# Sliding-window attention beside a GELU layer: the first chunk's logits copied from PSUM bank by bank, and another order of the pieces

## The chip, the core and the metric

The kernel runs on one core of a Trainium2 chip. The metric is the device time of one execution in microseconds (us), the median of several runs. The engines of the core are TensorE (PE in the profile, its weight loads PEld), VectorE (DVE), ScalarE (ACT), GpSimd (POOL) and SyncE (SP, which here issues DMA transfers). Each works through its own list of instructions in order and waits on semaphores for the others.

## The reference

The input `x` has 2048 rows of 640 numbers in bf16. It is normalised (`xn`), and the output is the sum of `x`, an attention over a few earlier rows, and a dense layer with GELU:

```python
xn = layernorm(x)                                  # [2048, 640]
q, k, v = split(xn @ wqkv)                         # 32 heads of 20 numbers
# row s looks at the 8 rows s, s-2, ..., s-14 of its own head
logits[h, s, w] = (q[h, s] . k[h, s - 2*w]) * 20**-0.5     # -1e9 where s - 2*w < 0
attn = softmax(logits, over w)
o[h, s] = sum over w of attn[h, s, w] * v[h, s - 2*w]
out = x + o @ wo + gelu(xn @ w1 + b1) @ w2 + b2    # w1: 640 x 1536, w2: 1536 x 640
```

## The kernel before

The 2048 rows are cut into four chunks of 512, and each chunk into four blocks of 128. The program is made of 626 named pieces, and the list `ORDER` at the top of the file gives the order in which they are emitted. Each engine keeps that order for its own instructions; nothing reorders them later. Semaphore waits are put in by the framework where a piece uses what an earlier one wrote. In a piece's name the first digit is the chunk.

The pieces that matter here:

- `st`, `rs`, `rc`, `xn`: statistics of the rows (VectorE L213, L215, for chunks 2 and 3 ScalarE passes `su` L225 and `sq` L232 that write to a scratch tile `trash`), the reciprocal deviation on ScalarE (L244, L247) and the normalised rows. `tp`, `tc` turn them so that columns lie on partitions (`xnT`).
- `ho`, `wa`, `wb`, `tb`: at the start, a small table for the heads, matmuls that fill time, and the bias rows turned through TensorE.
- `pj` (L333) and, for chunk 0, `ga` to `ge` and `hj` (L346, L377): the projections to `qT`, `kT`, `vT`. TensorE adds them up in PSUM, four banks in turn, shared with the GELU layer's first product. `pc`, `gc`, `hc` copy them out on ScalarE (L397, L370, L392), and each such copy frees a bank. `pad` (L402 to L406) copies the last 14 columns of the chunk before in front of `kT` and `vT`; `pad11` (L404) is that of chunk 1's `kT`.
- `qk` (L430): VectorE multiplies a block's queries by the eight shifted windows of keys into the big tile `prod`. `pa`, `pb` (L465, L471) fold it, and `lg` (L480) sums it over a head's numbers on TensorE: the logits `L`, a PSUM tile of [128, 8 offsets, 128] in f32, which is two banks, offsets 0 to 3 in one and 4 to 7 in the other. There are four such products, one a chunk; "first logits" and "second logits" are those of chunks 0 and 1.
- the softmax: `cp` copies `L` to the bf16 tile `e`; `mask`; `m` and `mx` find and subtract the maximum (L527, L529, L538); `ex` is the exponential on ScalarE (L543); `ss` the sum (L527, L529); `ri` its reciprocal as a logarithm and an exponential on ScalarE (L552, L553); `at` the product (L558), named `attn`. The exponentials and logarithms use another table of ScalarE than GELU, so a table load (L170) stands between them. Chunk 0 does all this in two halves `a` and `b` of 64 columns (`PARTS`), the other chunks in one.
- `xe`: transfers on SP that spread `attn` to all rows of a head. `av`, `ac`, `ad`, `ot` (L584 to L607): the weighted sum of values.
- `f1` (L614) and `ge` (L630): the GELU layer's first product and GELU, to `hT`. `t` (L696) turns the second product and the output projection into the tile `T`, `u` (L699) adds the bias, `ut` turns it by DMA and `ud` (L708) adds it to the output in DRAM, to which `xp` (L300) wrote `x` before. The last chunk ends in another way: `o` (L652), `dl`, `dh` (L664) and `dd`; `xb` adds its bias rows into `x`.
- `ldx`, `ld2`, `ldo`: loads on SP of later rows of `x`, of `w2` and of `wo`.

In chunk 0 `cp0b` is a VectorE copy of columns 64 to 127 of all eight offsets, and `cp0a` a ScalarE copy of columns 0 to 63 of all eight, so each reads from both banks. In the order they stand as `cp0b cp0a`.

Of the kernel before, what the change touches and what calls it, by code (L numbers as in the profile page):

```python
# [16 lines left out]
S, D, F, H, W, DIL = 2048, 640, 1536, 32, 8, 2  # L17
# [14 lines left out]
PARTS = (2, 1, 1, 1)  # L32
# [5 lines left out]
COLS = ((0, 2), (2, 4), (4, 5))  # L38

ORDER = """  # L40
pad01 pad02 st00a st00 sum1 ho rs00 neg1 xn00a sq1 xn00b tp00a wa tp00b wb tc00a tc00b rs01 ga xn01a gb2 xn01b tp01a
gb3 st02a tb tp01b tc01a gb4 st02 tc01b gd gc0 st03a ge rs02 st03 hj101 b1 xn02 rs03 gc4 xn03 gc1 tp02 st12a tp03
hc101 st11a hj100 tc03 st10a st12 tc02 hj102 st13a hc100 hj010 st10 hc102 st13 hj200 st11 rs1 hj110 hc200 rc1 qk01
xn10 hj012 hc110 tc10 hj011 pk xn11 hj111 hc012 tc11 hc010 qk00 hc011 hj112 hc111 f10_2 hc112 xn13 f10_0 xn12 tc13
qk02 f10_1 tc12 ge0_0 f10_5 ldx qk03 f10_11 ge0_5 f10_3 ge0_11 ge0_2 pj101 ge0_3 pa00 pj112 pc101 ge0_1 pj104 pc112
xp2 pa01 su20 pj110 xp0 pc104 ld2 su22 pj102 pc110 pb01 pj100 su21 hj201 su23 pc102 pb04 pj103 ng2 pc100 hc201 pj114
sq22 lg0 pc114 ldo pj111 cp0b cp0a sq21 mask pj113 m0b pc103 m0a pj124 pc111 mx0a pc113 mx0b t000 pad11 qk11 pj120
ex0b hj202 ex0a hj210 pc120 sq23 ss0a hj211 pc124 ss0b sq20 pj122 qk13 hc202 rs2 f10_7 hc211 pc122 t040 ri0b f10_8
ri0a rc2 qk12 hc210 f10_4 f11_1 ge0_7 xn21 qk10 f11_3 ge0_4 tc21 xn20 pj121 ge1_3 tc20 t041 ge1_1 pa11 f11_9 ge0_8
xn23 hj212 pc121 tc23 t001 xn22 pa10 f10_6 hc212 tc22 ge1_9 f11_10 ge0_6 at0a at0b f10_9 ge1_10 pb11 xe01 su33 xe03  # L50
t002 xe00 ge0_9 pj123 pad21 su32 pb14 pj210 xe02 su31 pj203 xp1 pc210 su30 lg1 t042 pc203 av01 cp1b f10_10 ng3 f11_5
pj212 ge1_5 av00 ac01 pc123 f11_0 cp1a ge0_10 pj204 pad12 ge1_0 m1 pc212 ac00 pj211 sq32 av02 pj202 sq30 t003 pc211
pc204 pj221 pc202 mx1 pj223 av03 ex1 pj222 sq31 t043 pj214 ss1 pc222 pc221 f11_2 ac03 ri1 pj213 pc214 sq33 at1 pj220
ac02 pc213 xe11 rs3 xe13 pj201 pc220 xe10 rc3 ad01 pj224 pc201 xe12 pc223 ad00 pj200 f12_9 pc200 ot00 xn33 f12_3 ot01
xn31 tc33 av11 t004 tc31 t044 u00 pc224 t010 u04 ut00 av13 ac11 t011 xn32 t012 t013 ud00 f11_11 av12 t014 t030 u01
t031 xn30 ac13 t020 tc30 t032 ac12 t021 ge1_11 t022 ge2_9 av10 t023 t024 t033 t034 ad11 ac10 f11_7 xb ot11 f12_2 ge1_7
qk22 pad31 ge2_3 f11_8 pad22 ge1_2 f11_6 u03 ut01 tc32 ge1_8 qk23 f13_1 ge2_2 ge1_6 pj310 f11_4 pc310 pa21 pj304 ge1_4
pj312 ad10 pj311 pc312 pc304 pj301 ot10 qk21 pj314 t140 pc314 t141 pc301 u02 pj302 qk20 pc311 ut02 t130 pj300 ut03
pj313 pc300 ut04 ud01 pa20 t142 pc313 f12_6 ud02 pb21 f13_4 ge2_6 ud03 pc302 t131 f13_0 pb24 t132 pj303 lg2 pc303 t133
ge3_1 qk33 t134 cp2b cp2a t143 ge3_0 u13 t144 pad32 m2 f12_0 mx2 t110 qk32 ex2 t111 f12_8 u14 pj321 ss2 ge2_0 t100  # L60
t101 qk30 f13_6 ri2 t102 t103 ge3_4 pa31 t112 ge2_8 t104 ge3_6 pc321 pj322 u10 at2 qk31 f13_2 xe20 xe21 f13_5 ge3_2
xe23 t113 ge3_5 xe22 pa30 f12_10 pc322 ut10 t120 f13_10 pb31 f12_4 ge3_10 ge2_10 f13_3 pb34 t114 f13_8 u11 ut11 ud10
lg3 ge3_8 t121 av21 cp3a f12_5 ge2_4 cp3b f12_7 ge2_5 pj323 ge2_7 m3 ac21 f13_7 mx3 av20 ex3 f12_1 t122 t123 ge3_7
t124 av23 ac20 ge3_3 ge2_1 o300 u12 t200 ut12 ud11 t230 ud04 ss3 t201 pj320 ac23 ri3 o301 pc323 av22 f13_9 t231 ge3_9
o320 pc320 o321 at3 ac22 o302 xe31 ut13 pj324 ad20 f12_11 pc324 ad21 t232 xe30 ge2_11 xe32 t202 ut14 ot21 f13_11 ot20
t203 av31 t204 t233 u20 t234 ut20 av30 t210 u23 ud12 xe33 t211 t212 t213 t214 ac30 t220 u21 ac31 t221 ge3_11 t222 av33
t223 t224 o310 u22 ud13 ud20 ut21 ud14 t240 ad30 o311 av32 t241 o312 t242 t243 t244 o303 u24 ud21 ut22 ud22 ut23 ot30
o330 ut24 ac32 o322 ud23 o313 ac33 o304 ad31 o331 ud24 o323 dl0 dh0 o314 ot31 dd0 o324 dl1 dh1 dd1 o332 dl2 o333 dh2
dd2 o334 ohi dl3 dlo dh3 dhi
""".split()  # L70


# [1 line left out]
def kernel(  # L74
# [16 lines left out]
    nc = tc.nc  # L91
# [48 lines left out]
    for c in range(2):  # L140
        cs = slice(c * F // 2, (c + 1) * F // 2)
# [32 lines left out]
    mask = consts.tile([H, W, MW], BF16, name="mask")  # L174
# [27 lines left out]
    tiles = {}  # L202
# [287 lines left out]
    def part(n, i):  # L490
        width = P // PARTS[n]
        return slice(i * width, (i + 1) * width), width

    def softmax_tile(key, n, shape, dtype):
        return get((key, n), lambda: smp.tile([P, PARTS[n]] + [s // PARTS[n] if s == P else s for s in shape], dtype, tag=key, name=key))
# [16 lines left out]
    def do_cp(n, i):  # L512

        e = softmax_tile("e", n, [W, P], BF16)
        if PARTS[n] == 1:
            ws = slice(W // 2 * i, W // 2 * (i + 1))
            nc.scalar.copy(e[:, 0, ws, :], tiles["L", n][:, ws, :])
        else:
            cs, width = part(n, i)
            (nc.vector.tensor_copy if i else nc.scalar.copy)(e[:, i, :, :], tiles["L", n][:, :, cs])  # L520

    def do_mask():
        e = tiles["e", 0][0:H, 0, :, 0:MW]
# [231 lines left out]
    for n in range(NCH):  # L755
# [34 lines left out]
        for i in range(2):  # L790
            piece(f"cp{n}" + "ab"[i], do_cp, n, i)
# [65 lines left out]
```

## Time and profile before

| what | value |
|---|---|
| median of 3 runs | 206.0 us (205.8 to 206.23) |
| the profiled execution | 205.97 us |
| its span, first to last instruction | 203.8 us |
| TensorE busy | 199.9 us, 98% |
| VectorE busy | 185.8 us, 91% |
| ScalarE busy | 128.9 us, 63% |
| GpSimd busy | 29.3 us, 14% |

The execution's own time is 2.1 us above its span; that rest lies outside the program's instructions. All times of rows are counted from the start of the span. In a timeline a row gives the start, the time to the end of the last instruction in it, the engine, the line, the operation, what is written and read, and the count; brackets give the engine's idle time before it and what ended that. Instructions of one engine overlap a little at their ends, so a row's length is up to 0.1 us more than the step from one start to the next. Matmuls of 512 columns stand 0.216 us apart, though each lasts 0.38.

### The profile page before, as it was taken

Reading aid. Unit: us, or ns where it says so; the run is one execution under the profiler, and the core shown is the slowest. Engines: PE = TensorE matmul, PEld = TensorE weight load, DVE = VectorE, ACT = ScalarE, POOL = GpSimd, SP = SyncE. Lnnn points to the kernel's source line nnn. Section 1 sums busy time; section 2 is a strip of 40 time slices with the busy share of each in tenths; the row PEclk is TensorE's granted clock in tenths of the full one; section 3 lists DMA queues with packets and bytes.
Section 4 is the critical chain, followed back from the end, with each engine's and each line's share of the span. In section 5 each row is a group of like instructions: output and inputs, shape, how many; then the busy total and the mean of one; then the engine's idle time right before and its main releaser. Section 6 shows DMA issues by size and latency. Waiting matters only on the chain.

```text
span 203.8 us, 2870 instructions
## 1 busy us (share of the span) xinstructions
PE 199.9 (98%) x1100; PEld 105.1 (52%) x1100; DVE 185.8 (91%) x160; ACT 128.9 (63%) x237; POOL 29.3 (14%) x34
## 2 busy tenths in 40 slices
PE   8999999999999999999999999999999999999994
PEld 3998456574544555444445544444434454444552
DVE  2889999699998999999999998999979999998871
ACT  5669899899896998657184445996379942230100
POOL 2000000000000400040420040000022713236210
PEclk9999999999999999999999999999999999999999
DMA  6997499900448781779399190003745899795851
GB/s 203 389 395 207 93 314 372 351 2 0 68 86 260 154 155 19 190 145 131 82 160 104 26 102 1 3 0 61 170 51 105 141 104 204 96 104 76 79 90 64
DMA packets 38430, 27.31 MB, mean 134 GB/s; under 512 B 25106, under 2 KB 34578, under 8 KB 38418
## 3 DMA queue, kind: packets, MB, share of 16 engines
q1 hardware_dynamic: 28016, 20.39, 35.3%
q0 software_dynamic: 10080, 6.56, 27.9%
q10 hardware_dynamic: 322, 0.20, 0.3%
q8 instruction: 8, 0.13, 0.3%
q14 instruction: 4, 0.03, 0.0%
HBM read 10.49 MB, written 4.59 MB: 74 GB/s over the span
## 4 chain that ended last, share of the span: by engine, by line
PE 84%; ACT 7%; DMA 4%; DVE 2%; SPq 1%; issue 1%
PE T L696 27%; PE hps L614 23%; PE pps L333 22%; PE lo L652 5%; DMA x_sb<-in_A_x_dram 4%; PE both L652 2%; DVE stats L213 2%; ACT xn L262 2%; PE gps L377 1%; PE hi L652 1%; ACT L170 1%; PE L L480 1%; ACT qT L392 1%; ACT e L543 1%; ACT kT L392 1%
## 5 line engine op out<-in xcount | busy, mean ns | idle before, releaser
L614 PE MATMUL hps<-xnT,w_sb 128*128 128x512 bf16 x240 | 56.2, 379 | 0.2 <-ACT hT L630 0.2
L430 DVE TENSOR_TENSOR prod<-qT,kT 128x5120 bf16<-128x5120 bf16 x16 | 44.6, 2821 | 1.3 <-ACT qT L397 1.0
L696 PE MATMUL T<-hT,w_sb 128*128 128x512 bf16 x180 | 44.6, 379 | 0.0
L614 PEld LDWEIGHTS <-w_sb 128*128 128x128 bf16 x240 | 23.4, 98 | 28.2 <-issue 0.5
L708 POOL DMA_DIRECT2D out_dram<-x_sb x15 | 20.8, 1485 | 65.7 <-DMA x_sb<-x_sb 65.6
L630 ACT ACTIVATE hT<-hps,bT 128x512 bf16<-128x512 f32 x36 | 23.7, 691 | 9.5 <-PE hps L614 9.3
L696 PEld LDWEIGHTS <-w_sb 128*128 128x128 bf16 x180 | 17.2, 98 | 20.9 <-issue 1.3
L584 DVE TENSOR_TENSOR prod<-vT,ax 128x5120 bf16<-128x5120 bf16 x8 | 22.4, 2821 | 1.9 <-PE L L480 1.1
L699 ACT ACTIVATE x_sb<-T,bT 128x512 bf16<-128x512 f32 x15 | 10.4, 693 | 21.6 <-PE T L696 19.2
L584 DVE TENSOR_TENSOR prod<-vT,x_sb 128x5120 bf16<-128x5120 bf16 x8 | 22.3, 2820 | 0.1
L595 POOL DMA_DIRECT2D prod<-prod x6 | 7.3, 1208 | 98.6 <-DVE prod L584 98.6
L170 ACT ACT_TABLE_LOAD x14 | 18.0, 1283 | 1.0 <-PEq L841 0.7
L471 DVE TENSOR_TENSOR prod<-prod 128x4096 bf16<-128x4096 bf16 x8 | 18.3, 2292 | 0.2
L333 PE MATMUL pps<-xnT,wq_sb 128*128 128x512 bf16 x75 | 18.5, 379 | 0.0
L696 PE MATMUL T<-oT,wo 128*128 128x512 bf16 x75 | 18.5, 379 | 0.0
L333 PE MATMUL pps<-xnT,wv_sb 128*128 128x512 bf16 x75 | 18.3, 379 | 0.0
L333 PE MATMUL pps<-xnT,wk_sb 128*128 128x512 bf16 x75 | 18.3, 379 | 0.0
L465 DVE TENSOR_TENSOR prod<-prod 128x4096 bf16<-128x4096 bf16 x8 | 18.1, 2288 | 0.1
L597 DVE TENSOR_TENSOR prod<-prod 128x2560 bf16<-128x2560 bf16 x10 | 14.6, 1485 | 0.0
L397 ACT CAST qT<-pps 128x512 bf16<-128x512 f32 x15 | 8.6, 582 | 7.2 <-PE pps L333 7.2
L333 PEld LDWEIGHTS <-wk_sb 128*128 128x128 bf16 x75 | 8.7, 118 | 7.7 <-issue 0.4
L333 PEld LDWEIGHTS <-wv_sb 128*128 128x128 bf16 x75 | 8.7, 117 | 7.6 <-issue 0.4
(96 smaller groups left out, 240.8 us busy)
## 6 DMA issues: line engine op xcount, KB each, us to landing
prod<-prod POOLq DMA_DIRECT2D x6, 640.0 KB, 6.5
ax<-attn SPq DMA_DIRECT2D x8, 256.0 KB, 4.3
x_sb<-attn SPq DMA_DIRECT2D x8, 256.0 KB, 4.2
w_sb<-in_B_w_dram SPq DMA_DIRECT2D x2, 960.0 KB, 11.3
out_dram<-x_sb SPq DMA_DIRECT2D x3, 640.0 KB, 5.0
w_sb<-in_B_w_dram SPq DMA_DIRECT2D x4, 480.0 KB, 7.2
out_dram<-x_sb POOLq DMA_DIRECT2D x15, 128.0 KB, 3.9
x_sb<-in_A_x_dram SPq DMA_DIRECT2D x2, 640.0 KB, 7.1
```

The lines of the kernel that those rows point to most:

```text
L170: nc.scalar.preload_act_table_set(name)
L333: nc.tensor.matmul(ps[:], lhsT=wqkv_p[which][:, ti, to, :], rhs=xnT[:, ti, :], start=(ti == 0), stop=(ti == KT - 1),)
L430: nc.vector.tensor_tensor(out=prod[:, j], in0=q[:, :, at].unsqueeze(1).to_broadcast([P, W, KT, P]), in1=window(k, at), op=ALU.mult,)
L465: nc.vector.tensor_tensor(out=low, in0=low, in1=high, op=ALU.add)
L471: nc.vector.tensor_tensor(out=first, in0=first, in1=rows[:, :, t * P : (t + 1) * P], op=ALU.add)
L584: nc.vector.tensor_tensor(out=prod[:, j], in0=window(qkv_tile(n, 2), slice(j * P, (j + 1) * P)), in1=ax_view(n)[:, j, :, :].unsqueeze(2).t ...
L597: nc.vector.tensor_tensor(out=low, in0=low, in1=high, op=ALU.add)
L614: nc.tensor.matmul(ps[:], lhsT=w1_sb[:, ti, ft * P : (ft + 1) * P], rhs=tiles["xnT", n][:, ti, :], start=(ti == 0), stop=(ti == KT - 1),)
L630: nc.scalar.activation(hT, tiles["hps", n, ft][:], ACT.Gelu_apprx_tanh, bias=bT[:, ft : ft + 1], scale=1.0)
L652: nc.tensor.matmul(out_ps(bl, hi), lhsT=lhs, rhs=rhs[:, CH:D] if hi else rhs[:, 0:CH], start=pc == 0 and k == 0, stop=pc == 4 and k == len ...
L696: nc.tensor.matmul(ps[:], lhsT=lhs, rhs=rhs, start=pc == 0 and k == 0, stop=pc == 4 and k == len(srcs) - 1)
L708: nc.gpsimd.dma_start(dst, src, accum_op=ALU.add)
```

## The change

`cp` now cuts the first chunk's logits by offsets instead of columns: `cp0a` (ScalarE) copies offsets 0 to 3 of all 128 columns, which is one bank, and `cp0b` (VectorE) offsets 4 to 7, the other bank. Each writes its four offsets into both 64-column halves of `e`, so the stretches that the two write lie interleaved in `e`. The sizes are the same: 512 numbers per partition each. The other chunks' copies, two on ScalarE by offsets, are what they were.

`ORDER` holds the same pieces in another order. The functions of the pieces are otherwise the same; behind line 520 the lines move up by three.

```diff
     def do_cp(n, i):
 
         e = softmax_tile("e", n, [W, P], BF16)
-        if PARTS[n] == 1:
-            ws = slice(W // 2 * i, W // 2 * (i + 1))
-            nc.scalar.copy(e[:, 0, ws, :], tiles["L", n][:, ws, :])
-        else:
-            cs, width = part(n, i)
-            (nc.vector.tensor_copy if i else nc.scalar.copy)(e[:, i, :, :], tiles["L", n][:, :, cs])
+        ws = slice(W // 2 * i, W // 2 * (i + 1))
+        copy = nc.vector.tensor_copy if i and PARTS[n] > 1 else nc.scalar.copy
+        copy(e[:, :, ws, :], tiles["L", n][:, ws, :].rearrange("p w (a c) -> p a w c", a=PARTS[n]))
```

Of the order, the start, and the stretch from the first logits `lg0` to the reciprocals `ri0`:

```diff
-pad01 pad02 st00a st00 sum1 ho rs00 neg1 xn00a sq1 xn00b tp00a wa tp00b wb tc00a tc00b rs01 ga xn01a gb2 xn01b tp01a
-gb3 st02a tb tp01b tc01a gb4 st02 tc01b gd gc0 st03a ge rs02 st03 hj101 b1 xn02 rs03 gc4 xn03 gc1 tp02 st12a tp03
+pad01 pad02 st00a st00 sum1 rs00 neg1 xn00a sq1 xn00b tp00a tp00b tc00a wa rs01 wb tc00b ga ho xn01a xn01b tb tp01a
+gb2 tc01a tp01b st03a gb3 tc01b gb4 st03 gd st02a rs03 ge st02 gc0 xn03 hj100 rs02 gc4 xn02 gc1 b1 tp03 st12a tp02
...
-sq22 lg0 pc114 ldo pj111 cp0b cp0a sq21 mask pj113 m0b pc103 m0a pj124 pc111 mx0a pc113 mx0b t000 pad11 qk11 pj120
-ex0b hj202 ex0a hj210 pc120 sq23 ss0a hj211 pc124 ss0b sq20 pj122 qk13 hc202 rs2 f10_7 hc211 pc122 t040 ri0b f10_8
-ri0a rc2 qk12 hc210 f10_4 f11_1 ge0_7 xn21 qk10 f11_3 ge0_4 tc21 xn20 pj121 ge1_3 tc20 t041 ge1_1 pa11 f11_9 ge0_8
+xp2 lg0 pc104 pj113 cp0b cp0a ldo pc102 pj111 mask m0b pc113 pc112 m0a hj202 pc111 mx0b pj124 mx0a t000 ex0a pj123
+sq23 hj210 pc124 ex0b f10_4 pad11 qk13 ss0a hc202 ss0b hc210 pc123 pj120 qk11 ri0a sq20 pj122 ri0b rs2 pj121 pc120
+at0a pc122 rc2 t040 qk12 f11_9 ge0_4 f10_8 xn20 qk10 hj211 pc121 tc20 xn21 t001 ge1_9 tc21 f10_7 hc211 ge0_8 pa11
```

The rest of the list is reordered in the same way, piece by piece; the four `lg`, the `av`, `ot`, `t`, `u` and `ud` keep their chunks' order.

More of the change, by code (lines that the diff above doesn't have):

```diff
@@ L40 @@
 ORDER = """
-pad01 pad02 st00a st00 sum1 ho rs00 neg1 xn00a sq1 xn00b tp00a wa tp00b wb tc00a tc00b rs01 ga xn01a gb2 xn01b tp01a
-gb3 st02a tb tp01b tc01a gb4 st02 tc01b gd gc0 st03a ge rs02 st03 hj101 b1 xn02 rs03 gc4 xn03 gc1 tp02 st12a tp03
-hc101 st11a hj100 tc03 st10a st12 tc02 hj102 st13a hc100 hj010 st10 hc102 st13 hj200 st11 rs1 hj110 hc200 rc1 qk01
-xn10 hj012 hc110 tc10 hj011 pk xn11 hj111 hc012 tc11 hc010 qk00 hc011 hj112 hc111 f10_2 hc112 xn13 f10_0 xn12 tc13
-qk02 f10_1 tc12 ge0_0 f10_5 ldx qk03 f10_11 ge0_5 f10_3 ge0_11 ge0_2 pj101 ge0_3 pa00 pj112 pc101 ge0_1 pj104 pc112
@@ L46 @@
-xp2 pa01 su20 pj110 xp0 pc104 ld2 su22 pj102 pc110 pb01 pj100 su21 hj201 su23 pc102 pb04 pj103 ng2 pc100 hc201 pj114
-sq22 lg0 pc114 ldo pj111 cp0b cp0a sq21 mask pj113 m0b pc103 m0a pj124 pc111 mx0a pc113 mx0b t000 pad11 qk11 pj120
-ex0b hj202 ex0a hj210 pc120 sq23 ss0a hj211 pc124 ss0b sq20 pj122 qk13 hc202 rs2 f10_7 hc211 pc122 t040 ri0b f10_8
-ri0a rc2 qk12 hc210 f10_4 f11_1 ge0_7 xn21 qk10 f11_3 ge0_4 tc21 xn20 pj121 ge1_3 tc20 t041 ge1_1 pa11 f11_9 ge0_8
-xn23 hj212 pc121 tc23 t001 xn22 pa10 f10_6 hc212 tc22 ge1_9 f11_10 ge0_6 at0a at0b f10_9 ge1_10 pb11 xe01 su33 xe03
@@ L51 @@
[L51 to L69, printed above, removed]
+pad01 pad02 st00a st00 sum1 rs00 neg1 xn00a sq1 xn00b tp00a tp00b tc00a wa rs01 wb tc00b ga ho xn01a xn01b tb tp01a
@@ new lines @@
+gb2 tc01a tp01b st03a gb3 tc01b gb4 st03 gd st02a rs03 ge st02 gc0 xn03 hj100 rs02 gc4 xn02 gc1 b1 tp03 st12a tp02
+st10a tc03 hj101 st13a hc100 st11a st10 tc02 hj102 st12 hj200 hc102 hc101 st13 st11 hj010 hc200 rs1 hj111 rc1 qk01
+xn10 hj011 hc111 tc10 xn11 hj110 pk hc010 tc11 qk00 hj112 hc011 hc110 hj012 hc112 hj201 hc012 xn13 f10_2 hc201 qk03
+tc13 xn12 f10_0 tc12 f10_5 ldx ge0_0 qk02 f10_1 ge0_2 f10_11 pj101 ld2 ge0_11 pa00 ge0_1 pj110 ge0_5 pc101 f10_3 pc110
+pa01 su20 pj114 ge0_3 su22 pj102 pb01 pc114 pj103 su21 su23 pj112 xp1 pc103 pb04 pj100 ng2 sq22 xp0 pj104 pc100 sq21
@@ new lines @@
+xp2 lg0 pc104 pj113 cp0b cp0a ldo pc102 pj111 mask m0b pc113 pc112 m0a hj202 pc111 mx0b pj124 mx0a t000 ex0a pj123
+sq23 hj210 pc124 ex0b f10_4 pad11 qk13 ss0a hc202 ss0b hc210 pc123 pj120 qk11 ri0a sq20 pj122 ri0b rs2 pj121 pc120
+at0a pc122 rc2 t040 qk12 f11_9 ge0_4 f10_8 xn20 qk10 hj211 pc121 tc20 xn21 t001 ge1_9 tc21 f10_7 hc211 ge0_8 pa11
+f11_1 ge0_7 xn22 f11_3 xn23 tc22 pa10 t041 ge1_1 f10_9 tc23 su33 f10_6 ge1_3 at0b pb11 xe00 f11_10 ge0_6 xe02 xe01
+hj212 ge1_10 t002 ge0_9 pb14 xe03 pj210 su32 pj203 pc210 su31 lg1 su30 f11_0 av00 ng3 hc212 f10_10 sq32 pj211 ge0_10
@@ new lines @@
+pad12 pc203 av02 t042 ac00 sq30 pj200 cp1a pc211 f11_5 pc200 av01 sq31 pj213 ge1_0 pj214 cp1b sq33 pj220 m1 pc214 ac01
+pc213 pj222 ge1_5 mx1 av03 t043 pj212 ex1 t003 pc212 pj202 ss1 pc222 pj224 ac02 ri1 f12_2 pc220 pc224 at1 pj204 rs3
+ac03 xe10 pj201 xe13 pc204 xe11 ad00 pj223 pc201 pc202 xe12 rc3 pj221 ot00 xn30 ad01 pc223 f11_11 xn32 f11_8 ot01 tc32
+av10 t004 t044 u00 pad21 t010 u04 ut00 av13 t011 xn31 tc30 t012 pad31 pc221 t013 tc31 ud00 t014 av11 t030 u01 t031
+xn33 t032 tc33 t020 ac13 ac11 t021 ge1_11 t022 av12 ge1_8 ac10 t033 t023 f11_4 t034 ac12 f11_6 u03 ut01 ad11 ge2_2
@@ new lines @@
+t024 ge1_4 pj303 ot11 qk22 pj311 pj300 pc311 ge1_6 f11_2 pc300 qk23 f12_6 ge1_2 pj302 ge2_6 pc303 f11_7 pa21 u02 pc302
+ut02 t130 pj304 ut03 ad10 pj312 pc304 ut04 ud01 ge1_7 f12_3 ot10 pc312 qk20 t140 ud02 ge2_3 pj314 ud03 f13_4 qk21 xb
+t141 t142 pj313 pj310 pc313 pa20 f13_0 pc310 pc314 t143 pb21 f12_9 pj301 pb24 t131 pc301 t132 t144 lg2 f13_3 cp2b qk30
+cp2a t133 ge3_0 t134 ge3_4 f13_6 u13 m2 t110 mx2 t111 qk31 ex2 t112 t113 u14 t114 pad22 t100 pa30 ge3_6 t101 ge3_3
+pj321 ge2_9 ss2 f12_4 t102 qk33 ri2 t103 pc321 f12_11 pad32 f13_1 at2 ge2_4 t104 qk32 xe22 xe20 f13_2 u10 xe21 ge3_1
@@ new lines @@
+f13_5 ge2_11 ut10 pa31 ge3_2 t120 f13_10 t121 pb31 xe23 f13_8 f12_0 ge3_8 ge3_5 pb34 f12_7 u11 ge3_10 ut11 ud10 f12_10
+ge2_0 lg3 f13_7 av21 pj322 ge3_7 ge2_10 f12_8 ge2_7 cp3b av20 t122 ac21 cp3a f12_5 pc322 pj323 ge2_5 m3 ac20 t123
+pc323 f12_1 mx3 av22 t124 ge2_1 ge2_8 pj320 u12 ut12 ud11 ud04 t200 av23 pj324 ex3 o300 ut13 t201 ss3 t230 f13_11 ac22
+ri3 t231 pc324 o301 pc320 ac23 t232 f13_9 at3 ge3_11 ad21 xe31 t233 xe33 t202 xe30 ad20 o310 o311 ut14 ot21 o312 ot20
+t203 av31 t204 t234 u20 ut20 t210 u23 ud12 ac31 t211 ge3_9 xe32 t220 av33 t212 o320 t213 t214 av30 t221 u21 t222 t223
@@ L70 @@
+t224 ac33 t240 u22 ud13 ud20 ut21 ud14 ac30 t241 t242 t243 ad30 o321 o322 av32 t244 o330 u24 ud21 ut22 ud22 ut23 o302
+ot30 ut24 o331 ac32 o332 ud23 o323 ad31 o313 o303 ud24 ot31 o314 o304 dl1 o324 dl0 dh1 dh0 dd1 o333 dl2 dd0 o334 dh2
+dd2 ohi dl3 dlo dh3 dhi
 """.split()
```

## Prediction

> **What bounds the kernel now.** I read the page first, then the engines' timelines around the first chunk's logits, then who waits for whom at L404 and L520. The page's part 1 (engine, busy us, share of the span, instructions):
>
> ```profile
> PE 199.9 (98%) x1100; PEld 105.1 (52%) x1100; DVE 185.8 (91%) x160; ACT 128.9 (63%) x237; POOL 29.3 (14%) x34
> ```
>
> TensorE is the bound: matmuls stand back to back from 0.78 us. Any idle time that an edit gives TensorE is added to the end, and what can be won is little. From the starts of its rows, the pauses between the first and second logits products are 0.34 us (43.24), 0.21 (44.53) and 0.10 (51.75), and one before them is 0.36 (23.75). But VectorE (91%) is close behind, and TensorE depends on it at four places, the logits products of L480. The second one, on TensorE (start, us, what):
>
> ```profile
> 61.79 1.24 PE L333 MATMUL pps<-xnT,wq_sb 128*128 128x512 bf16 x5
> 62.96 0.62 PE L480 MATMUL L<-prod,head_of 128*32 128x512 bf16 x8
> ```
>
> and VectorE, from the first chunk's softmax to that product:
>
> ```profile
> 39.36 0.76 DVE L538 TENSOR_TENSOR e<-e,ax 128x512 bf16<-128x512 bf16 x2
> 40.29 2.83 DVE L430 TENSOR_TENSOR prod<-qT,kT 128x5120 bf16<-128x5120 bf16 x1 [0.17 <-ACT kT L404]
> 43.03 0.42 DVE L527 TENSOR_TENSOR ax<-e 128x256 f32<-128x256 bf16 x1
> 44.87 2.82 DVE L430 TENSOR_TENSOR prod<-qT,kT 128x5120 bf16<-128x5120 bf16 x1
> ...
> 58.22 4.61 DVE L471 TENSOR_TENSOR prod<-prod 128x4096 bf16<-128x4096 bf16 x2
> 63.67 2.83 DVE L584 TENSOR_TENSOR prod<-vT,ax 128x5120 bf16<-128x5120 bf16 x1 [0.83 <-ACT trash L225]
> ```
>
> From 40.29 to 62.83 VectorE has no gap; TensorE takes the result at 62.96, 0.1 us after it is ready. So whatever delays VectorE's multiply at 40.29 delays the second logits, and with them the end, by all but 0.1 us. That multiply was let go by ScalarE's copy of the key padding, L404. ScalarE there:
>
> ```profile
> 37.12 0.59 ACT L520 CAST e<-L 128x512 bf16<-128x512 f32 x1 [0.70 <-DVE e L520]
> 37.60 0.83 ACT L232 ACTIVATE trash<-x_sb,neg 128x640 bf16<-128x640 bf16 x1
> ...
> 38.42 0.57 ACT L397 CAST qT<-pps 128x512 bf16<-128x512 f32 x1
> 38.89 1.08 ACT L397 CAST kT<-pps 128x512 bf16<-128x512 f32 x2
> 40.01 0.25 ACT L404 COPY kT<-kT 128x70 bf16<-128x70 bf16 x1
> 40.27 1.28 ACT L170 ACT_TABLE_LOAD   x1
> 41.57 1.15 ACT L543 ACTIVATE e<-e 128x512 bf16<-128x512 bf16 x2
> 42.62 0.57 ACT L397 CAST vT<-pps 128x512 bf16<-128x512 f32 x1
> 43.09 0.83 ACT L232 ACTIVATE trash<-x_sb,neg 128x640 bf16<-128x640 bf16 x1
> ```
>
> The padding copy goes ahead of the table load and the two exponentials. Differences of starts give the time of a step in a queue: copy 0.47 to 0.48 us, square pass 0.82, table load 1.30, exponential 0.52, padding copy 0.25.
>
> **The two copies by bank.** One VectorE copy (0.69 us) and one ScalarE copy (0.59) stay, each still of 512 numbers per partition, so I leave their durations. Today ScalarE's waits 0.70 us for VectorE's. The built program of the changed kernel still holds that wait: ScalarE's copy waits for the count of VectorE's, for the two now write interleaved stretches of `e`. So this edit is worth 0. If the copies did run side by side, ScalarE would start at 36.42, but the third key projection's copy needs matmuls that end at 38.6; the padding copy would then come some 0.5 us sooner. Bounds: 0 to -0.5 us; I take 0, as the wait stands in the program.
>
> In the Trainium skill, page "PSUM — Partial Sum Buffer", section "PSUM bank collisions raise a hardware error", two engines must not touch one bank (and the same partitions) at once, while different banks are free. By that rule alone the wait of 0.70 us would go; the trace has it with shared banks, and no run here shows it without.
>
> **The new order around the first softmax.** After VectorE's copy the changed ScalarE queue reads: copy of `e`, `qT` copy, three `kT` copies, table load, exponential, square pass, `vT` copy, exponential, and only then the padding copy `pad11`, and behind it `qk13`, now VectorE's first multiply, waits for it (the program has the wait). From the same 37.12:
>
> - five copies 0.48 + 0.47 + 3 x 0.48 = 2.39, to 39.51 (the last one's matmuls end near 38.6, so it isn't held up);
> - table 1.30 to 40.81; exponential 0.52 to 41.33; square pass 0.82 to 42.15; `vT` 0.47 to 42.62; exponential 0.52 to 43.14; padding copy 0.25 to 43.39; about 0.03 until VectorE starts: 43.42.
>
> VectorE has nothing else: it stands idle from 40.12 to 43.42, 3.3 us in the place of 0.17. Its multiply starts 3.13 us later. From it to the last fold the two orders hold the same 17 instructions on VectorE (four multiplies L430, six steps of the sums L527 and L529, four folds L465 and L471, two `attn` L558, one `nmr` L252), today 22.54 us without a gap. The second logits become ready at 62.83 + 3.13 = 65.96 instead of 62.83.
>
> **What TensorE does meanwhile.** ScalarE's next step is `ri0a` (L552), which needs the sum after that multiply: 43.42 + 2.74 (multiply) + 0.92 (L527 and L529, 43.95 less 43.03) = 47.1. Queued behind it are the other L552 pair, a square pass, `rs2` and the `vT` copies that free TensorE's PSUM banks. From today's starts: 0.46 + 0.82 + 0.43 + 0.46 + 0.57 = 2.74, to 49.85. TensorE's list after the first logits (36.27) holds eight groups of five 512-column matmuls (8 x 1.08), fifteen of 256 columns (1.64) and six of `T` (1.30), 11.6 us, to 47.85; the next group `f11_9` needs that bank. TensorE idles 2.0 us. It then gets to the second logits at 35.73 + 26.58 (today's 62.96 - 35.73 less the pauses of 0.65; the same 143 matmuls in both orders) + 2.0 + 0.2 (a pause behind the `hT` copy that follows the table load) = 64.5, and waits 1.5 us more for VectorE.
>
> So the second logits start at about 66.0 instead of 62.96: +3.0 us. The 143 matmuls' pauses of today (0.65) vanish in that figure; they aren't won again.
>
> **Start and rest.** At the start `ho`, the fillers `wa` and `wb` and the blocks' order move, and `tb` comes earlier, where it can wait up to 0.25 us for the bias rows. None of it counts: the first logits at 35.73 start on VectorE's string 15.45 to 35.54 (unbroken), and that hangs on the loads of `x` landing at 10.66 and the same statistics behind them; the same 252 matmuls precede. Without that cover the 0.25 would be paid. On SP the residual writes `xp` now stand together behind the `w2` loads; `T` first needs the first of those loads at 39.54, and it lands some 7 us after its issue at 28.65, now sooner. On POOL `xb` and some of the accumulations `ud` change places; POOL is busy 14%, and what they serve, the last chunk's sums and the buffers of `u`, comes after 87 us. I cost all this at 0, at most 0.3. After the second logits both orders give VectorE equal lists between the products; three more `T` matmuls (0.65 us) stand ahead of the third, which today starts 0.25 us after VectorE is done (119.82 + 4.62 = 124.44; L480 at 124.69). So VectorE's margin grows, and TensorE's rows show no pause there that could be won back: +0, up to +1 if a transfer comes late, about one in five.
>
> **Sum.** +3.0 to +3.1 on the profiled execution: 205.97 + 3.05 = 209.0 us (span 203.8 + 3.05 = 206.9, with the same 2.1 us around it). The median of the runs, 206.0, agrees with that execution.
>
> **The rivals.**
> 1. *Side by side*: the copies don't wait for each other. Against it: the program's wait. Sooner by 0.5 us: 208.5. Chance 0.04.
> 2. *The other side, faster*: `qk13` isn't held by the padding copy, since the fourth block's window reads no padding. It decides if the wait is met at the third `kT` copy, 39.5, instead of at the padding copy. Then VectorE goes on at 40.12, 0.17 sooner than today, and the second logits come up to 0.27 us sooner, TensorE's pauses of 0.65 being gone: 205.7. For it: nothing in that multiply's data needs the padding. Against it: today `qk11`, which reads none either, has the row `[0.17 <-ACT kT L404]`. Chance 0.05.
> 3. *TensorE slows down after its pause*: the fillers at the start (ten of 512 columns and three of 128 take 4.75 us, 0.43 us each against 0.216 later) show a half-speed TensorE after idling. Should 2 us of idling bring that back, 4.75 us at half speed lose some 2.4 us; 1.5 of them lie in the second wait that TensorE has anyway, so +0.9 to +1.1: 210.0. For it: only that start, after idling of unknown length. Against it: the rows after today's pauses are at full speed, but none of these is over 0.36 us; the profile's PEclk can't tell, for it reads 9 in the first slice too, where the rows show half speed. Chance 0.05.
>
> The Trainium skill, page "TensorE: Matmul & The Clock Gate", Part 1, has the clock drop after an idle window of about 3.4 us; by it a 2 us pause would keep full speed and the sum would stay 209.0. No row here tests it.
>
> **How the numbers follow.** Forecast 0.84, of it a fifth with up to 1 us of late transfers; rivals 0.04, 0.05 and 0.05; no measurable difference (within 0.2%, 0.4 us, about what a measurement of this kernel tells from none) 0.02. Slower: 0.84 + 0.04 + 0.05 = 0.93; faster 0.05; same 0.02. The range goes from rival 1 with 0.2 us of error in its steps, 208.3, to rival 3 with as much, 210.2.
>
> **What would show it.** Right: VectorE idle some 3.2 us ahead of a multiply near 43.4, let go by the padding copy; a pause of TensorE of 2 us near 48 to 50 let go by a `vT` copy, another of 1.5 us before the second L480, near 66; the second L480 to the end as long as today (138.1 us to the last matmul's end at 201.09). Wrong: ScalarE's copy of `e` starting with VectorE's; the multiply at 40.1; a second L480 before 63.5; or TensorE rows at half speed behind 50.

## The result, and the profile after

| | median | range of the runs |
|---|---|---|
| before, 6 runs | 206.0 us | 205.8 to 211.07 |
| after, 6 runs | 209.21 us | 208.8 to 209.41 |

The changed kernel is slower: after over before is 1.0154, with a 95% interval of 1.0141 to 1.0168, about 3.2 us. (The 211.07 fell in a disturbed state of the chip; the ratio leaves such runs out.) The profiled execution after took 209.10 us with a span of 207.0, against 205.97 and 203.8.

Part 1 of the page after, in the columns shown before:

```profile
PE 199.6 (96%) x1100; PEld 105.0 (51%) x1100; DVE 186.1 (90%) x160; ACT 126.8 (61%) x235; POOL 29.4 (14%) x34
```

No engine has over 0.3 us more to do, and ScalarE has 2.1 us less (12 table loads of 1.28 us instead of 14); TensorE's share falls from 98% to 96%. The time is lost in waiting, and part 5 of the page (the group, its count, busy us and mean ns, then the idle time before it and what ended most of it) names both places:

```profile
L611 PE MATMUL hps<-xnT,w_sb 128*128 128x512 bf16 x240 | 56.9, 379 | 2.0 <-ACT vT L397 2.0
L430 DVE TENSOR_TENSOR prod<-qT,kT 128x5120 bf16<-128x5120 bf16 x16 | 44.6, 2820 | 4.6 <-ACT kT L404 3.6
```

VectorE's multiplies waited 3.6 us for the key padding of L404, and the GELU layer's first product 2.0 us for a `vT` copy. Lines behind L520 carry numbers three lower than before (the copy of `e` is L517, the exponential L540). ScalarE's timeline after, from the copy of the logits on:

```profile
37.02 0.59 ACT L517 CAST e<-L 128x512 bf16<-128x512 f32 x1 [0.49 <-DVE e L517]
37.50 0.59 ACT L397 CAST qT<-pps 128x512 bf16<-128x512 f32 x1
37.98 1.58 ACT L397 CAST kT<-pps 128x512 bf16<-128x512 f32 x3
39.58 1.28 ACT L170 ACT_TABLE_LOAD   x1
40.88 0.63 ACT L540 ACTIVATE e<-e 128x512 bf16<-128x512 bf16 x1
41.41 0.81 ACT L232 ACTIVATE trash<-x_sb,neg 128x640 bf16<-128x640 bf16 x1
...
42.23 0.56 ACT L397 CAST vT<-pps 128x512 bf16<-128x512 f32 x1
42.69 0.63 ACT L540 ACTIVATE e<-e 128x512 bf16<-128x512 bf16 x1
43.22 0.24 ACT L404 COPY kT<-kT 128x70 bf16<-128x70 bf16 x1
...
47.27 0.26 ACT L549 ACTIVATE ax<-ax 128x64 f32<-128x64 f32 x1 [2.57 <-DVE ax L526]
...
49.39 1.06 ACT L397 CAST vT<-pps 128x512 bf16<-128x512 f32 x2
```

The copy of 70 numbers now stands behind the table load and both exponentials and starts at 43.22 instead of 40.01. VectorE's timeline shows who waits for it:

```profile
39.15 0.75 DVE L535 TENSOR_TENSOR e<-e,ax 128x512 bf16<-128x512 bf16 x2
43.49 2.83 DVE L430 TENSOR_TENSOR prod<-qT,kT 128x5120 bf16<-128x5120 bf16 x1 [3.59 <-ACT kT L404]
...
61.43 4.61 DVE L471 TENSOR_TENSOR prod<-prod 128x4096 bf16<-128x4096 bf16 x2
66.88 2.83 DVE L581 TENSOR_TENSOR prod<-vT,ax 128x5120 bf16<-128x5120 bf16 x1 [0.84 <-PE L L480]
```

And TensorE's shows how that wait travels: back through ScalarE's sum and `vT` copies to a full set of PSUM banks at 48, then through the logits at 66.

```profile
47.15 0.81 PE L693 MATMUL T<-hT,w_sb 128*128 128x512 bf16 x3
50.01 2.32 PE L611 MATMUL hps<-xnT,w_sb 128*128 128x512 bf16 x10 [2.05 <-ACT vT L397]
52.50 1.25 PE L377 MATMUL gps<-xnT,wv_sb 128*128 128x256 bf16 x10 [0.17 <-ACT hT L627]
...
66.09 0.61 PE L480 MATMUL L<-prod,head_of 128*32 128x512 bf16 x8 [1.22 <-DVE prod L471]
```

From the first logits product to the second TensorE took 27.24 us before (35.73 to 62.96) and 30.46 after (35.63 to 66.09): 3.2 us more. From the second to the end of the last matmul both take 138.13 us. The loss lies in this one stretch.

### The profile page after: what moved, and what is told of

It reads as the page before. It is cut to its first block, busy times and chain, and to the rows that moved or that the text cites. A ratio compares the mean times of both kernels' runs of the same rounds, so it can differ in the third digit from the quotient of the medians.

```text
span 207.0 us, 2861 instructions
## 1 busy us (share of the span) xinstructions
PE 199.6 (96%) x1100; PEld 105.0 (51%) x1100; DVE 186.1 (90%) x160; ACT 126.8 (61%) x235; POOL 29.4 (14%) x34
## 4 chain that ended last, share of the span: by engine, by line
PE 81%; DVE 11%; ACT 3%; DMA 2%; issue 1%; POOL 1%; POOLq 0%
PE T L693 25%; PE hps L611 20%; PE pps L333 19%; DVE prod L430 5%; PE lo L649 5%; PE gps L377 5%; DMA b_rt<-in_B_b_dram 2%; PE both L649 2%; DVE prod L471 2%; DVE prod L465 2%; PE hi L649 1%; PE L L480 1%; PE gps L346 1%; ACT kT L397 1%; ACT e L540 1%
## 5 line engine op out<-in xcount | busy, mean ns | idle before, releaser
L611 PE MATMUL hps<-xnT,w_sb 128*128 128x512 bf16 x240 | 56.9, 379 | 2.0 <-ACT vT L397 2.0
L705 POOL DMA_DIRECT2D out_dram<-x_sb x15 | 19.7, 1452 | 86.5 <-DMA x_sb<-x_sb 86.4
L397 ACT CAST kT<-pps 128x512 bf16<-128x512 f32 x15 | 8.5, 603 | 7.9 <-PE pps L333 7.9
L333 PEld LDWEIGHTS <-wq_sb 128*128 128x128 bf16 x75 | 8.8, 117 | 7.5
```

The lines of the kernel that those rows point to most:

```text
L333: nc.tensor.matmul(ps[:], lhsT=wqkv_p[which][:, ti, to, :], rhs=xnT[:, ti, :], start=(ti == 0), stop=(ti == KT - 1),)
L611: nc.tensor.matmul(ps[:], lhsT=w1_sb[:, ti, ft * P : (ft + 1) * P], rhs=tiles["xnT", n][:, ti, :], start=(ti == 0), stop=(ti == KT - 1),)
L705: nc.gpsimd.dma_start(dst, src, accum_op=ALU.add)
```

## The experiments

My theory: the place of `pad11` in ScalarE's list costs the 3 us, the copies by bank cost and bring nothing, and the rest of the new order is neutral. The rivals: the copies share the loss; the rest of the order costs or gains time; the fourth block's multiply truly needs the padding. Eight kernels ran, and the kernel before ran again beside them, with a median of 206.18 us beside e1 to e4 and of 206.29 beside e5 to e8. Ratios are against these runs. "Interval" below is from the start of the first logits product to that of the second, in the profiled execution, and doesn't depend on what comes before it.

| kernel | median us | ratio (95%) | interval us |
|---|---|---|---|
| before | 206.18, 206.29 | 1 | 27.24 |
| e1, copies alone | 206.12 | 0.9995 (0.9984 to 1.0006) | 27.24 |
| e2, order alone | 209.54 | 1.0153 (1.0126 to 1.0179) | 30.47 |
| e3, after, padding early | 205.69 | 0.9986 (0.9961 to 1.0010) | 26.96 |
| e4, before, padding late | 208.34 | 1.0104 (1.0084 to 1.0125) | 29.48 |
| e5, before's order, copies by bank, a tile a bank | 205.92 | 0.9984 (0.9971 to 0.9997) | 26.61 |
| e6, after, a tile a bank | 209.10 | 1.0128 (1.0111 to 1.0146) | 30.05 |
| e7, e6 with padding early | 205.54 | 0.9960 (0.9946 to 0.9974) | 26.61 |
| e8, after, padding behind | 206.07 | 0.9991 (0.9975 to 1.0007) | 27.19 |

In all of them 138.13 us lie between the second logits product's start and the last matmul's end.

**e1 and e2: the change in two halves.** e1 is the kernel before with the diff of `do_cp` alone, e2 the kernel before with the new `ORDER` alone.

> The copies by bank alone, in the order of before. Theory (the loss is the place of the padding copy pad11 in ScalarE's queue): as before, 206.0 us within 0.3, ScalarE's copy of e still starting at VectorE's end, 37.1. Rival A (the copies by bank cost or gain by themselves): over 0.4 us away from before, with copies longer than 0.69 and 0.59 us, or with the wait of 0.70 gone. A second rival (the order as a whole) also says 206.0 here.

> The new order alone, copies by column halves as before. Theory: 209.2 us within 0.3, like the changed kernel, with VectorE idle some 3.5 us ahead of the multiply at 43.5. Rival A (copies by bank): near 206.0. Rival B (the order as a whole, in places other than the padding copy): 209.2 as well; the next run parts it from the theory.

The whole loss is in the order. e2 has after's interval, 30.47 against 30.46, and after's ratio, 1.0153 against 1.0154; its median of 209.54 lies just above the range expected, as before's was 0.2 us higher beside it. (Its profiled execution was about 1 us late from the start on, behind the load of the query weights; the interval doesn't hold that.) In e1 the two copies stand as before, VectorE's and then ScalarE's:

```profile
36.43 0.69 DVE L517 CAST e<-L 128x512 bf16<-128x512 f32 x1 [0.86 <-PE L L480]
```

```profile
37.15 0.59 ACT L517 CAST e<-L 128x512 bf16<-128x512 f32 x1 [0.70 <-DVE e L517]
```

The wait of 0.70 us is untouched although the two read different banks.

**e3 and e4: one piece moved, both ways.** e3 is after with the padding copy ahead of the softmax's table load; e4 is before with the padding copy, and the multiply that follows it, behind the exponentials.

```diff
 e3, on after
-... hj202 pc111 mx0b pj124 ... f10_4 pad11 qk13 ss0a
+... hj202 pc111 pad11 mx0b pj124 ... f10_4 qk13 ss0a
 e4, on before
-... t000 pad11 qk11 pj120 ex0b hj202 ex0a hj210
+... t000 pj120 ex0b hj202 ex0a pad11 qk11 hj210
```

> The changed kernel with one piece moved back: pad11 stands behind the last kT copy and ahead of the table load. Theory: VectorE's multiply starts near 40.1 instead of 43.5, TensorE's pauses of 2.05 and 1.2 us go, the second logits start near 62.8 instead of 66.1; 205.8 us (205.5 to 206.1). Rival B (other moves of the order cost the 3 us): stays above 208.

> The kernel before with pad11 and the qk11 behind it moved behind the two exponentials, nothing else. Theory: the table load and two exponentials (1.30 + 2 x 0.52) now lie ahead of the padding copy: the multiply starts near 42.5 instead of 40.29, the second logits 2.1 us later; 208.1 us (207.8 to 208.4). Rival B: 206.0, as the rest of the order is that of before.

Moving one small copy in the changed kernel takes the loss away. e3's ScalarE and VectorE:

```profile
39.94 0.25 ACT L404 COPY kT<-kT 128x70 bf16<-128x70 bf16 x1
40.21 1.28 ACT L170 ACT_TABLE_LOAD   x1
```

```profile
40.22 2.83 DVE L430 TENSOR_TENSOR prod<-qT,kT 128x5120 bf16<-128x5120 bf16 x1
```

The multiply starts as soon as VectorE is free. With the interval at 26.96, 0.28 us shorter than before's, and the ratio not to be told from 1, the rest of the new order costs nothing. It may gain a little: the ratio's interval goes down to 0.9961 (0.8 us), and ten of e3's twelve runs are shorter than the shortest of before's 24 beside it (205.89). e4 makes the loss in the old order. The multiply is 2.5 us late (42.79 instead of 40.29, of which 0.18 was there at the first logits already), the interval 2.24 longer:

```profile
42.79 2.83 DVE L430 TENSOR_TENSOR prod<-qT,kT 128x5120 bf16<-128x5120 bf16 x1 [2.48 <-ACT kT L404]
```

```profile
65.39 0.61 PE L480 MATMUL L<-prod,head_of 128*32 128x512 bf16 x8 [1.67 <-DVE prod L471]
```

It is less than after's 3.2 because only the table load and the exponentials stand ahead of the padding copy there, not also the square pass and a `vT` copy.

**e5, e6 and e7: where ScalarE's wait comes from.** The two banks of `L` become two PSUM tiles of one bank each; the copies, the order (of before in e5, of after in e6, of e3 in e7) and the layout of `e` stay.

```diff
-        L = psL.tile([P, W, P], F32, tag="L", name="L")
-        tiles["L", n] = L
+        tiles["L", n] = L = [psL.tile([P, W // 2, P], F32, tag=f"L{h}", name="L") for h in range(2)]
...
-                        L[j * H : (j + 1) * H, W // 2 * h : W // 2 * (h + 1), :],
+                        L[h][j * H : (j + 1) * H, :, :],
...
-        copy(e[:, :, ws, :], tiles["L", n][:, ws, :].rearrange("p w (a c) -> p a w c", a=PARTS[n]))
+        copy(e[:, :, ws, :], tiles["L", n][i][:].rearrange("p w (a c) -> p a w c", a=PARTS[n]))
```

The filler matmuls, `tb` and the last chunk's output, which share that memory, take the same two tiles.

> The order of before, copies by bank, and the logits L as two PSUM tiles of one bank each instead of one of two banks; e is written in the same interleaved stretches. Theory (what held ScalarE's copy back is that both copies read one PSUM tile, not the interleaving in e): the wait of 0.70 goes, both copies start within 0.2 us of each other, the padding copy and the multiply behind it come 0.6 us sooner, the second logits 0.5 us sooner; 205.5 us (205.2 to 205.8). Rival (the reason given in the prediction, interleaved stretches of e): the wait stays, 206.0. Second rival: copies that run at once slow each other, longer than 0.75 and 0.65 us, and the gain is under 0.2 us.

> The changed kernel with the same two PSUM tiles. Theory: the copies run side by side and the padding copy comes 0.5 us sooner, though still behind the table load; the multiply near 43.0 instead of 43.5; 208.6 us (208.3 to 208.9). Rival (with the copies side by side the new order is right): 206.0 or less.

> The changed kernel with two PSUM tiles and the padding copy ahead of the table load. Theory: both losses are gone and TensorE has no pause over 0.2 us behind the first logits; 205.3 us (205.0 to 205.7), as fast as the order of before with two tiles, for the rest of the order moves nothing. Rival (the new order is better elsewhere): over 0.3 us faster than that.

In e5 the wait is gone and the copies run side by side, ScalarE's and VectorE's:

```profile
36.62 0.59 ACT L516 CAST e<-L 128x512 bf16<-128x512 f32 x1
```

```profile
36.70 0.69 DVE L516 CAST e<-L 128x512 bf16<-128x512 f32 x1 [0.85 <-PE L L479]
```

Neither is longer than alone (0.59 and 0.69 us before). `e` is still written in interleaved stretches, so the wait came from the one PSUM tile that both read. The Trainium skill, page "PSUM — Partial Sum Buffer", section "PSUM bank collisions raise a hardware error", lets different banks be read at once; e5 agrees. The gain is 0.63 us of the interval, but a ratio just below 1: 0.9984 is 0.33 us, and the median of 205.92 lies above the 205.2 to 205.8 expected. The mechanism came as expected, the gain in the whole time smaller.

For e6 208.6 us (208.3 to 208.9) was expected and 209.10 measured: its interval is 0.41 us shorter than after's, where 0.5 was expected, and its ratio 0.0026 (0.5 us) lower, though the intervals of the two ratios overlap. So copies side by side don't make the new order right; VectorE still stands idle for the padding, until 43.24:

```profile
43.24 2.83 DVE L430 TENSOR_TENSOR prod<-qT,kT 128x5120 bf16<-128x5120 bf16 x1 [3.73 <-ACT kT L404]
```

e7 undoes that as well and is the best version, faster than both kernels:

```profile
39.57 2.83 DVE L430 TENSOR_TENSOR prod<-qT,kT 128x5120 bf16<-128x5120 bf16 x1
```

```profile
62.34 0.61 PE L479 MATMUL L<-prod,head_of 128*32 128x512 bf16 x8
```

Its interval equals e5's, 26.61. But by the medians it is 0.38 us under e5, more than the 0.3 us that was set as the mark of the rival, and ten of e5's twelve runs are longer than the longest of e7's eight (205.72). With e3 this makes two pairs in which the new order, its padding copy put early, comes out 0.4 to 0.5 us shorter by the medians. So the rest of the order doesn't look neutral, as the theory had it, though the intervals of the ratios don't part e7 from e5. In the profiled executions e7 is ahead of e5 at the first logits already (35.73 against 36.03) and equal behind them, but e3 isn't ahead of before there (35.97 against 35.73). What the gain comes from is open; no run moves the pieces of the start alone.

**e8: does the multiply need the padding?** The same copy, moved the other way: directly ahead of the first block's multiply, `qk10`, which alone of the chunk's four reads it.

```diff
-... f10_4 pad11 qk13 ss0a ... qk12 ... xn20 qk10
+... f10_4 qk13 ss0a ... qk12 ... xn20 pad11 qk10
```

> The changed kernel with pad11 moved the other way, behind qk13, qk11 and qk12 and ahead of qk10, the one multiply whose window reads the padding. Theory: a multiply waits for the padding copy only because that was emitted ahead of it; now the first three do not, the first starts near 40.1; ScalarE's padding copy waits for the third multiply instead, some 0.5 us of that reaches the second logits: 206.2 us (205.8 to 206.6). Rival (the multiply needs something else that comes only at 43.4, the exponentials or the vT copy): 209.2.

The loss goes here too (206.07). The profiled execution is the longest of the ten runs, 209.68 us. It came some 4 us late to the first logits (39.56), so its rows are read among themselves alone:

```profile
43.09 0.75 DVE L535 TENSOR_TENSOR e<-e,ax 128x512 bf16<-128x512 bf16 x2
43.76 2.82 DVE L430 TENSOR_TENSOR prod<-qT,kT 128x5120 bf16<-128x5120 bf16 x1
```

VectorE goes on without a pause, though ScalarE's table load and exponentials stand where they stood. The data of the fourth block's multiply don't need the padding. It waits only when the padding copy was emitted ahead of it. The one multiply that does read the padding now waits for it, and the second logits product 0.48 us for VectorE:

```profile
54.61 2.83 DVE L430 TENSOR_TENSOR prod<-qT,kT 128x5120 bf16<-128x5120 bf16 x1 [0.32 <-ACT kT L404]
```

## Why the prediction was right

The forecast was 209.0 us (208.3 to 210.2), slower with 0.93; measured were 209.21 and, for the profiled execution, 209.10. By its steps:

- **Copies by bank, worth 0:** right, e1 (0.9995). But the reason given was wrong. Not "interleaved stretches of `e`" hold ScalarE back, but the PSUM tile that the two copies share: e5 keeps the stretches, takes the shared tile away and loses the wait. The profile of before could have told it: there the two copies wrote separate halves of `e` and waited 0.70 us all the same. The bound of -0.5 us for copies side by side had the right size: -0.63 in e5, -0.41 in e6.
- **ScalarE's queue ahead of the padding:** forecast 43.42, VectorE idle 3.3 us; measured 43.49 and 3.59. From the table load on the sum is exact (3.91 us forecast and measured). It is the three `kT` copies that were mis-sized: 3 x 0.48 = 1.44 against 1.60 (37.98 to 39.58), not held up by their matmuls, which end at 38.53. The row of before, two copies from 38.89 to 40.01, 0.56 each, already said so. The copy of `e` began 0.10 earlier with the whole program, so the two differences nearly cancel in the time of 43.49; that it is within 0.07 us of the forecast is in part luck.
- **VectorE's 17 instructions:** forecast to end at 65.96; the folds end at 61.43 + 4.61 = 66.04. No gap opened.
- **TensorE's pauses:** forecast 2.0 behind a `vT` copy, 0.2 behind an `hT` copy, 1.5 before the second logits; the trace has 2.05, 0.17 and 1.22. The chain back through the sum, ScalarE and the PSUM banks was right. The pause before the logits came out smaller, since TensorE was busy until 64.87 (63.63 + 1.24). By starts of rows, as the prediction counts, the first two pauses are 2.21 us (47.80 to 50.01) and 0.33 (52.17 to 52.50), 0.34 more than the 2.2 forecast, so TensorE came to the logits later than 64.5. The logits' start, 66.09 against 66.0, is set by VectorE whatever the pauses before it are.
- **Start and rest, 0:** right. The first logits came at 35.63, 0.10 sooner; `tb` did wait 0.26 us for the bias rows, where up to 0.25 was allowed, and nothing followed from it. After the second logits not 0.01 us differs. One remark was wrong: VectorE's margin at the third logits doesn't grow. VectorE ends its folds at 128.28 (123.66 + 4.62) and TensorE starts them at 128.47, 0.19 later, against 0.25 before; the three `T` matmuls ahead make them 0.65 us later, and VectorE comes 0.71 us later too.
- **Rival 1, side by side:** not in this kernel, which keeps the wait. e6 shows what it would have given, 0.41 us by the interval and 0.5 by the ratios, about as priced.
- **Rival 2, `qk13` not held:** not in this kernel. e8 shows that its argument on the data holds and the emitted order decides: where the padding copy isn't ahead, the multiply goes on at once. In e8 no gain over before can be told: the 0.3 us that the rival priced (205.7) lies within the ratio's interval (0.9975 to 1.0007), and so does none at all. There the fourth multiply's wait of 0.32 us stands in the place of before's 0.17 at the first.
- **Rival 3, half speed after the pause:** not in the profiled execution. The ten matmuls behind the 2.05 us pause take 2.32 us, 0.216 us apart. The Trainium skill's page "TensorE: Matmul & The Clock Gate", Part 1, with its idle window of about 3.4 us, agrees for this pause. The other runs leave the rival open. The mean granted clock is 0.992 in three of after's six runs (209.20, 209.23 and 209.41 us) and in one of e2's four (209.40), while it is at least 0.998 in 48 of the 49 runs of before beside the experiments. An estimate: 3.4 us at half speed lose 1.7 us of clock, and 1.7 of 207 is 0.008. No trace of these four runs was kept, so where the low clock lay isn't known. Their times lie among those of the two kernels' other runs (208.80 to 209.85), so it cost nothing that can be told, where the rival had +0.9 to +1.1.

So the sum was right because what it rests on is one late row of VectorE that sets the second logits, and VectorE had no gap behind it to take the lateness up.

## What to carry to other kernels

When an order is changed, look for the small instruction that slides behind a long one in another engine's queue: here a copy of 0.24 us behind a table load, two exponentials, a square pass and a `vT` copy cost 3.2 us, and putting it back (e3), or behind the work that doesn't need it (e8), took all of it away. Here a framework's wait followed what was emitted and the tile, not the elements: a multiply waited for padding that it doesn't read (e8), and two engines that read different banks of one PSUM tile took turns until each bank was a tile of its own (e5). A step on an engine with no gap up to the next handover moves the end by its full delay, so it can be added up from rows, each with the step of its own kind of copy.

## What the runs showed that was not expected

A stretch of half speed followed a pause of TensorE that was shorter than 3.4 us. In the profiled execution of e8 TensorE waited at the start for a load. Its timeline (pause in brackets) and busy times by windows (window, then for each engine busy us and count, the granted clock, the DMA share and GB/s):

```profile
8.69 0.58 PE L346 MATMUL gps<-xnT,wq_sb 128*128 128x128 bf16 x6 [2.57 <-DMA wq_sb<-in_A_wqkv_dram]
```

```profile
8.70:9.00 0.30, 0.30 (x6) 0.30 (x6) 0.00 (x0) 0.00 (x0) 0.00 (x0) 1.00 1.06 393
9.00:12.40 3.40, 3.40 (x37) 3.40 (x36) 2.36 (x8) 1.52 (x5) 0.00 (x0) 0.51 1.06 395
12.40:14.00 1.60, 1.60 (x26) 1.60 (x25) 1.31 (x5) 0.79 (x4) 0.00 (x0) 0.98 1.07 402
```

After 2.57 us of waiting the clock stays full for 0.3 us, is half for 3.4 us and then full again. In the 3.4 us ahead of the half-speed stretch (5.60 to 9.00) TensorE was busy for 0.83 us. Around the pause of 2.05 us in the kernel after, any stretch of 3.4 us holds at least 1.36 us of work (3.41 less 2.05), and in the profiled execution nothing of the kind follows. The Trainium skill, page "TensorE: Matmul & The Clock Gate", Part 1, gives an idle window of about 3.4 us; the half-speed stretch has that length, but the pause ahead of it was shorter. This is one execution, and no run was made to find the limit: that the pause brought the half speed, and how much work in a window prevents it, isn't shown. Rival 3 may have been nearer than the prediction's reading of that page made it.
